# Channel attention with a gelu FFN: v's splits one per step through DRAM, the seven-product scheme in first steps, softmax in finer pieces

## The chip, the cores and the metric

One core of one Trainium2 chip. The metric is the device time of one execution in microseconds; the time of a kernel is the median of several runs. All arithmetic is float32: every product of the main loops is made in three TensorE passes over operands split in a high and a low part (hi x hi, hi x lo, lo x hi), in the type fp32r.

## The reference

```python
B, N, C = 4, 6080, 256; d_ff = 2048
qn = q / (norm(q, axis=1) + 1e-6);  kn = k / (norm(k, axis=1) + 1e-6)   # per channel, over all N
s = kn.transpose(0, 2, 1) @ qn / tau                                    # 256 x 256 per batch
a = softmax(s, axis=-1)
x = (v @ a).reshape(B * N, C)
out = gelu(x @ w_in) @ w_out
```

## The kernel before, in words

**The algebra.** The 256 x 256 matrix a is folded into w_in: per batch, w = a @ w_in (256 x 2048) is made once, and the main loop does gelu(v @ w) @ w_out. v comes transposed (channels on the partitions).

**Groups and steps.** The main loop has 24 groups (b, p): batch b of 4, pair p of 6, each of two blocks of n tokens (n = 512, 480 for p = 5). A group has NU = 8 steps u, each for 256 of the 2048 columns of w. "First step" means u = 0, "second step" u = 1, "border" the change from one group to the next. A step's *first products* are the 2 x 2 block product v @ w in seven products of 128 x 128 with 128 x n (Winograd's form of Strassen's scheme, `first_products`, called do0 to do6 in the order `ORDER`, line 542). They go into two PSUM banks, h0 and h1, in turn; ScalarE copies two partial sums (p1, p5) and u2, VectorE adds them (h<-h,u and h<-h,p), and ScalarE applies gelu: twice per block (gh, rounded, and g, full), VectorE giving gl = g - gh.

**Second products.** gelu's result times w_out is a step late: while step i does its first products, the second products of step i-1 go in between, three matmuls after each do. In a step of the scheme (`strassen`, line 555, which leaves out u = 0) two of gelu's four blocks are kept whole in x, `sums` (line 586) forms the sums of blocks from it on VectorE (x<-x), ScalarE casts them to gh1 (768 columns) and gh0 (1024), VectorE makes gl1 and gl0, and the second products are 12 matmuls of 512 columns and 21 of 256 into the banks c10, c11, c00, p0, p1 and c01. After a plain step (u = 0) they are 24 of 512 columns into c10, c11, c00 and c01. With the 21 first matmuls of 512 that is 33 + 21 small, or 45.

**The end of a group.** Over eight steps the banks add up. c10 and c11 are copied out in the last second products. Then `combine` (line 763) takes p0 and p1 out (a ScalarE copy osb<-p, two VectorE osb<-p,osb, two osb<-osb,p) and `merge` (line 778) adds c00 and c01 to that (osb<-c,osb) and stores. Until merge 0 has read c00, the next group can't write there.

**What sets the order.** From group (0,1) on each of PE, VectorE and ScalarE keeps the program's order (`InOrder`, line 129). A table of jobs, `at(step, slot, job)`, puts side work behind the do of a slot (0 to 5), behind a step's products (6) or behind everything (EDGE = 8). The side work is:
- for the next group's v: `load_v`, four sums of its blocks (`v_sum`, line 516), and seven splits (`v_split`, ScalarE's cast vh, VectorE's vl = v - vh), straight into the operands that the next group's products read. An operand is free when the product of the same number in the last step has read it, so the splits of before stand in the last step and in the next group's first step (line 984);
- for the next batch: loads and splits of q and k (`split_qk`, hl<-raw,hl), their products in bursts of 8 matmuls added to sacc, the norms, and `softmax` (line 341) in the steps 36 to 39 of each batch's 48, followed by `w_part` (a @ w_in, 12 matmuls) and `w_split` (weight sums hl<-hl, wh, wl) in the steps 41 to 50;
- for each step: loads of wo and ws (w_out in two parts, and its sums) two steps and one step ahead (`ahead`, line 899).

All DMAs are issued by SP, in program order.

Of the kernel before, what the change touches and what calls it, by code (L numbers as in the profile page):

```python
# [17 lines left out]
P = 128  # L18
# [47 lines left out]
def channel_attention_gelu_ffn(ctx, tc, qk, kqt, vt, tau, w_in, w_out, out):  # L66
# [274 lines left out]
    def softmax(first):  # L341
# [39 lines left out]
        dve.reciprocal(out=r, in_=z)  # L381

# [121 lines left out]
    def load_v(b, p):  # L504
        t0, n = PAIRS[p]
        raw = pv.tile([P, NCT, 2 * NT], F32, name="v_raw")
        nc.sync.dma_start(out=raw[:, :, :2 * n],
                          in_=vt[:, b * N + t0:b * N + t0 + 2 * n].rearrange("(t p) n -> p t n", p=P))
        vraw[b, p] = raw
# [6 lines left out]
    def v_sum(b, p, i):  # L516
        n = PAIRS[p][1]
        x = v_blocks(b, p)
        if i == 0:
            vts[b, p] = [pv.tile([P, NT], F32, name=f"vs{k}") for k in range(4)]  # L520
        ts = [t[:, :n] for t in vts[b, p]]
        to, x0, x1 = ((0, x[0, 1], x[0, 0]), (2, x[1, 1], x[0, 1]), (1, x[1, 1], ts[0]), (3, x[1, 0], ts[1]))[i]
        dve.tensor_tensor(out=ts[to], in0=x0, in1=x1, op=ALU.subtract)

    def v_split(b, p, i):
# [3 lines left out]
        if (b, p) == (0, 0) and i == B12:  # L529
            src = x[0, 1]  # L530
        if src is None:
            src = vts[b, p][i - T1][:, :n]
# [22 lines left out]
    def strassen(b, p, u):  # L555
        return u > 0 and (b, p) > (0, 1) and (b, p, u) != (B - 1, NP - 1, NU - 1)
# [106 lines left out]
    def plain_products(b, p, u):  # L663
# [9 lines left out]
        for j in (1, 0):  # L673
# [14 lines left out]
    def second_products(b, p, u, blocks):  # L688
# [89 lines left out]
    def merge(b, p, c):  # L778
# [4 lines left out]
        parts = ((0, n // 2), (n // 2, n)) if last and c == NCT - 1 else ((0, n),)  # L783
        for lo, hi in parts:
# [78 lines left out]
    for i in (B11, B21, B12, B22):  # L863
        deque(v_split(0, 0, i), 0)
# [49 lines left out]
    for b in range(1, B):  # L914
        start, num, den = (8, 5, 2) if b == 1 else (4, 14, 5)
# [16 lines left out]
    EDGE = 8  # L932

    for (b, k), s in bursts.items():
# [10 lines left out]
        for m in range(NCT):  # L945
            at(s + m, EDGE, lambda b=b, k=k, m=m: burst(b, k, m))
# [5 lines left out]
    for b in range(1, B):  # L952
        base = (b - 1) * NP * NU
        for i in range(2 * NCT * NSC):

            def norm(b=b, i=i, step=base + 8 + i):
# [3 lines left out]
                at(step + 1, 2, lambda: next(gen, None))  # L960
            at(base + 8 + i, EDGE, norm)

        def soft(step=base + 36):
            gen = softmax(False)
            next(gen)
            spread(gen, step, 12, 10 + EDGE, 22, 26, 20 + EDGE)
        at(base + 36, EDGE, soft)
        for g in range(NWG):
            at(base + 39 + 2 * g, EDGE if g == 0 else EDGE + 1, lambda b=b, g=g: load_win(b, g))
            for m in range(NCT):  # L970
                at(base + 41 + 2 * g + m, EDGE, lambda b=b, g=g, m=m: w_part(b, g, m))
# [4 lines left out]
    for b in range(B):  # L976
        for p in range(NP):
            nxt = (b, p + 1) if p + 1 < NP else (b + 1, 0)
            base = (b * NP + p) * NU
            if nxt[0] < B:  # L980
                at(base + 1, EDGE, lambda nxt=nxt: load_v(*nxt))
                for i in range(4):
                    at(base + 3 + i, 6, lambda nxt=nxt, i=i: v_sum(*nxt, i))
                for i, (hi, lo) in enumerate(((1, 2), (2, 3), (3, 4), (5, 6), (6, 10), (10, 11), (11, 12))):

                    def vs(nxt=nxt, i=i, step=base + NU - 1, lo=lo):
                        gen = v_split(*nxt, ORDER[i][1])
                        next(gen)
                        spread(gen, step, lo)
# [83 lines left out]
```

## Time and profile before

| | |
|---|---|
| median of 3 runs | 2174.5 us (2173.92 to 2175.94) |
| the profiled execution | 2174.69 us |
| its span, first to last instruction | 2172.9 us |
| mean granted TensorE clock | 1.00 |
| PE, PEld, DVE, ACT, POOL busy | 99%, 84%, 80%, 75%, 0% |
| chain that ended last, by engine | PE 87%, DVE 7%, ACT 4%, issue 1% |
| DMA | 352.18 MB, mean 162 GB/s |

PE is TensorE's matmul stream, PEld its weight loads (beside it), DVE VectorE, ACT ScalarE, SP the engine that issues the DMAs. All times are microseconds from the start of the span. A row of the timeline has start, duration, engine, line, operation and the names out<-in; the line is 138 for nearly all, as one helper issues everything, so rows are told apart by their tiles. A row of the windows has a stretch of time, its length, and the busy time and instruction count of PE, PEld, DVE, ACT and POOL in it, then the granted clock, the share of DMA time and GB/s. In a row of groups stand the count, the busy time, and the mean of one in nanoseconds; in a row of DMA issues the count, the size of one and the median time to landing. The durations of neighbouring instructions on one engine overlap a little: what one adds to a queue is the distance of starts, its pitch.

### The profile page before, as it was taken

How to read it: one execution, taken by the hardware profiler on the slowest of the kernel's cores; microseconds unless marked ns; L12 is line 12 of the kernel's file. 1: busy time of each engine (PE TensorE's matmuls, PEld its weight loads, DVE VectorE, ACT ScalarE, POOL GpSimd, SP SyncE). 2: the span in 40 equal slices, each digit the busy share in tenths (PEclk: the TensorE clock that was granted, in tenths of full speed). 3: DMA queues.
4: the chain of work that ended last, by engine and by line, in shares of the span. 5: the costliest groups of instructions: out<-in, count | busy, mean ns of one | idle time of the engine just before them, and what ended most of it. 6: DMA issues, size and time to landing. Idle time of an engine off the chain costs nothing.

```text
span 2172.9 us, 29906 instructions
## 1 busy us (share of the span) xinstructions
PE 2152.8 (99%) x11061; PEld 1822.7 (84%) x11061; DVE 1734.9 (80%) x2732; ACT 1622.5 (75%) x2692; POOL 1.3 (0%) x8
## 2 busy tenths in 40 slices
PE   9999999999999999999999999999999999999999
PEld 8777888887888888888888888888888888888888
DVE  6997788877788788887788878888778777777776
ACT  5767778867777787786777778887677777677675
POOL 0000000000000000000000000000000000000000
PEclk9999999999999999999999999999999999999999
DMA  9545655544344555553434545554344333333332
GB/s 381 180 150 199 213 184 199 183 161 146 136 144 145 176 204 180 199 202 128 140 135 141 173 168 202 184 205 163 106 146 144 118 129 114 127 128 115 125 119 95
DMA packets 100547, 352.18 MB, mean 162 GB/s; under 512 B 10288, under 2 KB 12464, under 8 KB 98352
## 3 DMA queue, kind: packets, MB, share of 16 engines
q1 hardware_dynamic: 100400, 350.27, 46.3%
q8 instruction: 87, 1.43, 0.3%
q14 instruction: 60, 0.49, 0.1%
HBM read 312.74 MB, written 37.49 MB: 161 GB/s over the span
## 4 chain that ended last, share of the span: by engine, by line
PE 87%; DVE 7%; ACT 4%; issue 1%; DMA 0%; DVEq 0%; ACTq 0%; POOL 0%; POOLq 0%
PE h L138 45%; PE c L138 33%; PE p L138 9%; DVE h L138 2%; DVE vl L138 2%; DVE x L138 1%; ACT gh L138 1%; DVE gl L138 1%; ACT x L138 1%; ACT vh L138 1%; ACT g L138 0%; DVE small L138 0%; ACT L138 0%; ACT p L138 0%; DVE osb L138 0%
## 5 line engine op out<-in xcount | busy, mean ns | idle before, releaser
L138 PE MATMUL c<-gh,wo 128*128 128x512 f32 (+3 forms) x2460 | 870.4, 364 | 0.4 <-DVE wo L138 0.4
L138 PE MATMUL h<-vh,wh 128*128 128x512 f32 (+1 forms) x1312 | 520.3, 397 | 12.9 <-DVE h L138 2.8
L138 PEld LDWEIGHTS c<-gh,wo 128*128 128x128 f32 x2460 | 462.2, 188 | 81.9 <-DVE wo L138 1.5
L138 PE MATMUL h<-vh,wl 128*128 128x512 f32 (+1 forms) x1312 | 513.5, 391 | 0.0
L138 PE MATMUL h<-vl,wh 128*128 128x512 f32 (+1 forms) x1312 | 513.5, 391 | 0.0
L138 ACT ACTIVATE gh<-h 128x512 fp32r<-128x512 f32 (+1 forms) x446 | 277.9, 623 | 238.2 <-DVE h L138 219.2
L138 PE MATMUL c<-gl,wo 128*128 128x512 f32 (+3 forms) x1230 | 443.8, 361 | 0.1
L138 DVE TENSOR_TENSOR gl<-x,gh 128x768 fp32r<-128x768 f32 (+3 forms) x306 | 329.8, 1078 | 63.5 <-ACT gh L138 63.3
L138 DVE TENSOR_TENSOR gl<-g,gh 128x512 fp32r<-128x512 f32 (+1 forms) x462 | 314.5, 681 | 49.3 <-ACT g L138 47.1
L138 DVE TENSOR_TENSOR h<-h,p 128x512 f32<-128x512 f32 (+1 forms) x368 | 251.4, 683 | 79.5 <-PE h L138 68.3
L138 ACT COPY p<-h 128x512 f32<-128x512 f32 (+1 forms) x368 | 213.7, 581 | 126.3 <-PE h L138 126.2
L138 PEld LDWEIGHTS h<-vh,wh 128*128 128x128 f32 x1312 | 247.0, 188 | 72.3 <-ACT p L138 9.2
L138 ACT CAST gh<-x 128x768 fp32r<-128x768 f32 (+3 forms) x306 | 286.8, 937 | 16.7 <-DVE x L138 11.7
L138 PEld LDWEIGHTS h<-vh,wl 128*128 128x128 f32 x1312 | 246.4, 188 | 51.9
L138 DVE TENSOR_TENSOR x<-x 128x256 f32<-128x256 f32 (+4 forms) x491 | 241.1, 494 | 52.5 <-ACT x L138 34.8
L138 PEld LDWEIGHTS h<-vl,wh 128*128 128x128 f32 x1312 | 246.7, 188 | 35.4
L138 ACT ACTIVATE g<-h 128x512 f32<-128x512 f32 (+1 forms) x446 | 271.6, 609 | 0.0
L138 PEld LDWEIGHTS c<-gl,wo 128*128 128x128 f32 x1230 | 231.0, 188 | 45.3 <-DVE gl L138 0.5
L138 ACT ACTIVATE x<-h 128x512 f32<-128x512 f32 (+1 forms) x306 | 182.3, 609 | 48.9 <-DVE h L138 47.8
L138 PE MATMUL p<-gh,ws 128*128 128x256 f32 (+1 forms) x918 | 210.2, 280 | 0.0
L138 DVE TENSOR_TENSOR h<-h,u 128x512 f32<-128x512 f32 (+1 forms) x184 | 125.8, 684 | 83.5 <-PE h L138 82.6
L138 PEld LDWEIGHTS p<-gh,ws 128*128 128x128 f32 x918 | 162.6, 189 | 6.8
(153 smaller groups left out, 2229.5 us busy)
## 6 DMA issues: line engine op xcount, KB each, us to landing
wo<-keep_out SPq DMA_DIRECT2D x184, 512.0 KB, 4.5
ws<-keep_sum SPq DMA_DIRECT2D x153, 512.0 KB, 3.7
raw<-qk SPq DMA_DIRECT2D x94, 512.0 KB, 4.5
raw<-kqt SPq DMA_DIRECT2D x72, 512.0 KB, 4.6
v_raw<-vt SPq DMA_DIRECT2D x20, 1024.0 KB, 5.0
out<-osb SPq DMA_DIRECT2D x40, 512.0 KB, 3.9
hl<-keep_in SPq DMA_DIRECT2D x12, 1024.0 KB, 5.4
raw<-w_in SPq DMA_DIRECT2D x8, 512.0 KB, 6.9
```

The lines of the kernel that those rows point to most:

```text
L138: r = op(*args, **kw)
```

## The change

**v through DRAM, one operand per step.** In step i of a group (i = 0 to 6) the operand ORDER[i] of the next group is split: ScalarE's cast into a buffer vp behind do5, VectorE's subtraction (in place, into v_raw or vs) behind do3 of the next step (for i = 0 behind do6), and two DMAs store both parts in DRAM. In the group's last step `v_fetch` loads operand i into vh and vl behind do i. The four sums stand in the steps 0, 2, 3 and 4 and the buffer v_raw is loaded a group earlier; group (0,0) does this for (0,1) too.

**The scheme in first steps.** `strassen` no longer leaves out u = 0, in the groups from (0,2) on, so that all 8 steps of 22 groups use it. Then c01's first products write only half of the bank, and `merge` of c01 adds that half. `combine` and `merge` move: the combine's two halves to slots 1 and 2 of the second step, merge 0 to slot 2, merge 1 to slot 3.

**Softmax in finer pieces, border work ahead of the last groups.** `softmax` yields at two more places, and its pieces stand at the slots 2, 3, 7 (step 37), 2, 5, 6 (step 38) and 7 (step 39). A new slot EARLY = 7 lies after do6 and ahead of the second products that are still left (p1 and c01): bursts, w_part and the softmax's matmuls go there, where they stood behind all of them. The second products of a scheme step are ordered c00, c00, p0, p0, p1, p1, c01 (c00, p0, c00, p1, p1, p0, c01 before). The norms move to steps with few q and k splits, and the first bursts start one step earlier.

```diff
     def strassen(b, p, u):
-        return u > 0 and (b, p) > (0, 1) and (b, p, u) != (B - 1, NP - 1, NU - 1)
+        return (b, p) > (0, 1) and (b, p, u) != (B - 1, NP - 1, NU - 1)
...
         dve.reciprocal(out=r, in_=z)
+        if not first:
+            yield
...
+        if not first:
+            yield
+        for m in range(NCT):
             dve.reduce_max(out=nms[:, m:m + 1], in_=ts[m], axis=AX.X, negate=True)
...
+        hi = pv.tile([P, NT], F32R, name="vp", bufs=2)
+        act.copy(out=hi[:, :n], in_=f32(src))
+        yield
+        dve.tensor_tensor(out=src, in0=f32(src), in1=f32(hi[:, :n]), op=ALU.subtract)
+        to = keep_v[p % 2][i]
+        nc.sync.dma_start(out=to[:, 0, :n], in_=f32(hi[:, :n]))
+        nc.sync.dma_start(out=to[:, 1, :n], in_=f32(src))
+
+    def v_fetch(b, p, i):
...
+        nc.sync.dma_start(out=f32(hi[:, :n]), in_=keep_v[p % 2][i][:, 0, :n])
+        nc.sync.dma_start(out=f32(lo[:, :n]), in_=keep_v[p % 2][i][:, 1, :n])
...
+        if c == NCT - 1 and all(strassen(b, p, u) for u in range(NU)):
+            parts = ((n // 2, n),)
...
-            at(s + m, EDGE, lambda b=b, k=k, m=m: burst(b, k, m))
+            at(s + m, EARLY, lambda b=b, k=k, m=m: burst(b, k, m))
...
-            spread(gen, step, 12, 10 + EDGE, 22, 26, 20 + EDGE)
-        at(base + 36, EDGE, soft)
+            spread(gen, step, 12, 13, 10 + EARLY, 22, 25, 26, 30 + EARLY)
+        at(base + 36, 2, soft)
...
-                for i, (hi, lo) in enumerate(((1, 2), (2, 3), (3, 4), (5, 6), (6, 10), (10, 11), (11, 12))):
+                for i, (step, slot) in enumerate(((0, 6), (2, 0), (3, 0), (4, 0))):
+                    at(base + step, slot, lambda nxt=nxt, i=i: v_sum(*nxt, i))
+                for i, (_, x) in enumerate(ORDER):
...
+                        spread(gen, step, 16 if i == 0 else 13)
+                    at(base + i, 5, vs)
+                fetch = [(i, i) for i in range(7)]
...
-                        spread(gen, step, 1)
+                        spread(gen, step, 2)
                         for c in range(NCT):
-                            at(step, 2, lambda c=c: merge(b, p, c))
-                    at(base + NU + 1, 0, end)
+                            at(step, 2 + c, lambda c=c: merge(b, p, c))
+                    at(base + NU + 1, 1, end)
```

Three places of the engines' orders show what moved. The first is VectorE in the second step of group (1,3): osb<-p and osb<-osb are the combine of the group before, osb<-c00 and osb<-c01 its merges, gl the low parts of gelu, sacc a burst's sum, hl the split of q and k, h<-h0,u2 what do3's gelu needs. Before:

```order
L138 TENSOR_TENSOR gl1_8918<-g_8919,gh1_8917 128x512
L138 TENSOR_TENSOR sacc_6603<-h0_8950,sacc_6603 128x512
L138 TENSOR_TENSOR gl0_8933<-g_8934,gh0_8932 128x512
L138 TENSOR_TENSOR osb_8973<-p0_8187,osb_8973 128x256
L138 TENSOR_TENSOR osb_8973<-p1_8202,osb_8973 128x256
L138 TENSOR_TENSOR osb_8973<-osb_8973,p1_8202 128x256 x2
L138 TENSOR_TENSOR osb_8973<-c00_8086,osb_8973 128x512
L138 TENSOR_TENSOR osb_8973<-c01_8098,osb_8973 128x512
L138 TENSOR_TENSOR hl_8987<-raw_8830,hl_8987 128x1024
L138 TENSOR_TENSOR h_9007<-h0_8977,u2_8994 128x512
```

After, with vs a sum of the next v:

```order
L138 TENSOR_TENSOR vs_9386<-v_raw_9278 128x512
L138 TENSOR_TENSOR x_9353<-x_9353 128x512
L138 TENSOR_TENSOR x_9353<-x_9353 128x256 x2
L138 TENSOR_TENSOR gl1_9389<-x_9353,gh1_9388 128x768
L138 TENSOR_TENSOR gl0_9391<-x_9353,gh0_9390 128x1024
L138 TENSOR_TENSOR osb_9427<-p0_8498,osb_9427 128x256
L138 TENSOR_TENSOR osb_9427<-p1_8511,osb_9427 128x256
L138 TENSOR_TENSOR hl_9425<-raw_9276,hl_9425 128x1024
L138 TENSOR_TENSOR osb_9427<-osb_9427,p1_8511 128x256 x2
L138 TENSOR_TENSOR osb_9427<-c00_8483,osb_9427 128x512
L138 TENSOR_TENSOR h_9447<-h0_9414,u2_9434 128x512
```

The scheme's x sums and its two wide gl now stand ahead of the combine, the hl split has moved from behind the merges to between the combine's halves, and h<-h0,u2 still follows merge 0, with merge 1 behind it.

The second is ScalarE in the same step, from its last gelu on; p1, p5 and u2 are the copies of the first products. Before:

```order
L138 ACTIVATE g_8934<-h1_8835 128x512
L138 COPY p1_8966<-h1_8962 128x512
L138 COPY osb_8973<-p0_8187 128x256
L138 COPY p5_8981<-h0_8977 128x512
L138 CAST hl_8987<-raw_8830 128x1024
L138 COPY u2_8994<-h1_8962 128x512
```

After:

```order
L138 ACTIVATE x_9353<-h1_9281 128x512
L138 CAST gh1_9388<-x_9353 128x768
L138 COPY p1_9406<-h1_9402 128x512
L138 CAST gh0_9390<-x_9353 128x1024
L138 COPY p5_9418<-h0_9414 128x512
L138 CAST hl_9425<-raw_9276 128x1024
L138 COPY osb_9427<-p0_8498 128x256
L138 COPY u2_9434<-h1_9402 128x512
```

The copy osb<-p0 that starts the combine was ahead of p5 and hl, and is behind both and behind the two casts gh1 and gh0.

The third is ScalarE around the exponentials (t0, t1) of batch 2's softmax, with the two table loads that they need. Before:

```order
L138 COPY p5_10470<-h0_10466 128x512
L138 COPY u2_10479<-h1_10455 128x512
L138 ACT_TABLE_LOAD
L138 ACTIVATE t0_10329,small_10328<-t0_10329,small_10328 128x256
L138 ACTIVATE t1_10331,small_10328<-t1_10331,small_10328 128x256
L138 ACT_TABLE_LOAD
L138 ACTIVATE gh_10492<-h_10490 128x512
L138 ACTIVATE g_10494<-h_10490 128x512
```

After:

```order
L138 ACTIVATE gh_11015<-h_11012 128x512
L138 ACTIVATE g_11017<-h_11012 128x512
L138 ACTIVATE x_11032<-h_11029 128x512
L138 CAST vp_11040<-vs_10625 128x480
L138 ACT_TABLE_LOAD
L138 ACTIVATE t0_10761,small_10760<-t0_10761,small_10760 128x256
L138 ACTIVATE t1_10763,small_10760<-t1_10763,small_10760 128x256
L138 ACT_TABLE_LOAD
L138 ACTIVATE x_11032<-h1_10962 128x512
L138 CAST gh1_11062<-x_11032 128x768
```

They were behind the step's copies, ahead of its first gelus; they are now between the last two gelus (x) of a step, behind one v cast.

More of the change, by code (lines that the diff above doesn't have):

```diff
@@ L505, in load_v @@
         t0, n = PAIRS[p]
-        raw = pv.tile([P, NCT, 2 * NT], F32, name="v_raw")
-        nc.sync.dma_start(out=raw[:, :, :2 * n],
+        raw = pv.tile([P, NCT, 2 * NT], F32R, name="v_raw")
+        nc.sync.dma_start(out=f32(raw[:, :, :2 * n]),
                           in_=vt[:, b * N + t0:b * N + t0 + 2 * n].rearrange("(t p) n -> p t n", p=P))
@@ L518, in v_sum, with v_first @@
         x = v_blocks(b, p)
[L519 to L523, printed above, removed]
+        ts = vts.setdefault((b, p), {})
+        to, x0, x1 = ((T1, x[0, 1], x[0, 0]), (T2, x[1, 1], ts.get(T1, x)), (T4, x[1, 0], ts.get(T2, x)),
+                      (T3, x[1, 1], x[0, 1]))[i]
+        x0, x1 = f32(x0), f32(x1 if i in (0, 3) else x1[:, :n])
+        ts[to] = pv.tile([P, NT], F32R, name="vs", bufs=2)
+        dve.tensor_tensor(out=f32(ts[to][:, :n]), in0=x0, in1=x1, op=ALU.subtract)
+    keep_v = [[pdram.tile([P, 2, NT], F32, name=f"keep_v{k}_{i}") for i in range(7)] for k in range(2)]
+    def v_first(i, name):
+        n = PAIRS[0][1]
+        src = v_blocks(0, 0)[{B11: (0, 0), B21: (1, 0), B22: (1, 1), B12: (0, 1)}[i]]
+        hi = pv.tile([P, NT], F32R, name=f"vh{name}")
+        lo = pv.tile([P, NT], F32R, name=f"vl{name}")
+        vops[0, 0, i] = hi, lo
+        act.copy(out=hi[:, :n], in_=f32(src))
+        dve.tensor_tensor(out=lo[:, :n], in0=f32(src), in1=f32(hi[:, :n]), op=ALU.subtract)
     def v_split(b, p, i):
@@ L528, in v_split @@
         src = {B11: x[0, 0], B21: x[1, 0], B22: x[1, 1]}.get(i)
-        if (b, p) == (0, 0) and i == B12:
-            src = x[0, 1]
         if src is None:
-            src = vts[b, p][i - T1][:, :n]
+            src = vts[b, p][i][:, :n]
+        hi = pv.tile([P, NT], F32R, name="vp", bufs=2)
+        act.copy(out=hi[:, :n], in_=f32(src))
+        yield
[4 more added lines that the diff above has]
+    def v_fetch(b, p, i):
+        n = PAIRS[p][1]
         hi = pv.tile([P, NT], F32R, name=f"vh{i}")
@@ L953, in channel_attention_gelu_ffn, with norm @@
         base = (b - 1) * NP * NU
-        for i in range(2 * NCT * NSC):
-            def norm(b=b, i=i, step=base + 8 + i):
+        split_at = {}
+        for k in range(FIRSTB if b == 1 else 0, NQS // NB):
+            for t in range(NB):
+                x = bursts.get((b, k - 1), bursts[b, k] - 3) + 1 + t
+                split_at[x] = split_at.get(x, 0) + 1
+        free = sorted(range(base + (9 if b == 1 else 2), base + 35), key=lambda x: (x % NU == 0, split_at.get(x, 0), x))
+        for i, x in enumerate(sorted(free[:2 * NCT * NSC])):
+            def norm(b=b, i=i, step=x):
                 gen = norm_part(b, *divmod(i, NSC))
@@ L959, in norm @@
                     next(gen)
-                at(step + 1, 2, lambda: next(gen, None))
-            at(base + 8 + i, EDGE, norm)
+                at(step, 2, lambda: next(gen, None))
+            at(x - 1, EDGE, norm)
         def soft(step=base + 36):
```

39 lines of the change are left out of this document (20 added, 19 removed).

## The prediction

> **What bounds the kernel now.** I read the page's busy shares first, then the windows cut at the starts of the 192 steps, then the timelines of the steps that are longer than their matmuls.
>
> ```profile
> span 2172.9 us, 29906 instructions
> PE 2152.8 (99%) x11061; PEld 1822.7 (84%) x11061; DVE 1734.9 (80%) x2732; ACT 1622.5 (75%) x2692; POOL 1.3 (0%) x8
> ```
>
> TensorE is busy 99% of the span, so time is gained only by fewer matmuls or by closing PE's few gaps, and lost wherever a new wait of PE appears. The next rows are step windows: a step in the scheme, a second step of a group (its second products are those of the plain first step), and the sums over all 22 first steps and all 22 second steps of the groups from (0,2) on.
>
> ```profile
> core 0: us, PE busy (x) PEld busy (x) DVE busy (x) ACT busy (x) POOL busy (x), PEclk, DMA share, GB/s
> 1954.23:1964.32 10.09, 10.09 (x57) 8.66 (x55) 7.51 (x12) 7.00 (x12) 0.00 (x0) 1.00 0.30 104
> 1933.71:1944.14 10.43, 10.43 (x47) 8.38 (x46) 8.11 (x14) 7.11 (x13) 0.00 (x0) 1.00 0.51 174
> sum 248.98, PE 244.90 PEld 200.87 DVE 226.87 ACT 222.23 POOL 0.00; mean PE 11.13 PEld 9.13 DVE 10.31 ACT 10.10 POOL 0.00
> sum 240.31, PE 240.30 PEld 196.80 DVE 186.52 ACT 162.10 POOL 0.00; mean PE 10.92 PEld 8.95 DVE 8.48 ACT 7.37 POOL 0.00
> ```
>
> The granted clock is 1.00 in every row. First steps take 248.98/22 = 11.32 us with VectorE busy 10.31 of it; second steps 10.92 with VectorE at 8.48. Where the matmuls of a step start tells the rest:
>
> ```profile
> 1954.23 0.40 PE L138 MATMUL h<-vh,wh 128*128 128x512 f32 x1
> 1954.46 0.40 PE L138 MATMUL h<-vl,wh 128*128 128x512 f32 x1
> 1960.45 0.28 PE L138 MATMUL c<-gh,wo 128*128 128x256 f32 x1
> 1960.56 0.28 PE L138 MATMUL c<-gl,wo 128*128 128x256 f32 x1
> ```
>
> Starts are 0.232 us apart for 512 columns and 0.116 for 256. So 33 x 0.232 + 21 x 0.116 = 10.09 for a scheme step and 45 x 0.232 = 10.44 for a plain one, as the windows have it. The first matmul into c00 comes 1960.45 - 1954.23 = 6.22 us into a step.
>
> **The change part by part.** The sum stands against the profiled execution's own 2174.69 us, 1.8 us more than its span and 0.2 above the median of 2174.5. A measurement of this kernel can tell about 0.2% (4.3 us) from no change.
>
> *1. Scheme in 22 first steps.* Each saves 10.43 - 10.09 = 0.34 us of matmul in the step after it: **-7.6**.
>
> *2. Waits in the first steps.* Their matmuls, counted at 0.232 and 0.116 (0.219 and 0.110 in the 480-column groups, with the bursts), come to 235.65 us; the windows' sum is 248.98. The 13.3 us between are waits behind the v splits that crowd VectorE and ScalarE there. With one split per step they go: **-13.3**. What is late next is the second step.
>
> *3. Waits in the second steps.* This decides. Before, the old group's combine and merge have a plain step's short VectorE queue ahead of them. Now the scheme's sums of the first step stand there. Of a group border of before and of a steady step:
>
> ```profile
> 1954.00 1.61 DVE L138 TENSOR_TENSOR x<-x 128x512 f32<-128x512 f32 x3 [0.75 <-ACT x L138]
> 1955.53 0.95 DVE L138 TENSOR_TENSOR gl<-x,gh 128x768 fp32r<-128x768 f32 x1
> 1956.73 1.23 DVE L138 TENSOR_TENSOR gl<-x,gh 128x1024 fp32r<-128x1024 f32 x1 [0.25 <-ACT gh L138]
> ...
> 886.21 0.88 DVE L138 TENSOR_TENSOR osb<-p,osb 128x256 f32<-128x256 f32 x2 [0.48 <-ACT osb L138]
> 887.13 0.75 DVE L138 TENSOR_TENSOR osb<-osb,p 128x256 f32<-128x256 f32 x2
> 887.92 1.29 DVE L138 TENSOR_TENSOR osb<-c,osb 128x512 f32<-128x512 f32 x2
> 889.12 1.22 DVE L138 TENSOR_TENSOR hl<-raw,hl 128x1024 fp32r<-128x1024 f32 x1
> 890.25 0.69 DVE L138 TENSOR_TENSOR h<-h,u 128x512 f32<-128x512 f32 x1
> ```
>
> In the border of before (its step begins at 884.32) merge 0 ends at 887.92 + 0.69 = 888.61, 4.3 us in, 1.9 ahead of c00's 6.22. In the steady step the last sum, gl of 1024, ends at 1957.96, 3.73 in. In the new order a v sum (0.69) stands ahead of the x sums and fills most of the idle 0.75, so I put gl's end at 3.8 to 4.2. Then the combine (0.88 + 0.75, with pitch 0.92 + 0.79) and merge 0 (0.69) give 4.2 + 0.92 + 0.79 + 0.69 = 6.6: c00 waits 0.4. That is so at 10 of the 21 borders, **+4**.
>
> At 8 borders, (0,3), (0,4), (1,2) to (1,4) and (2,2) to (2,4), a q/k split falls into the second step. VectorE's part (889.12 to 890.25, 1.13) now lies between the halves of the combine, and ScalarE's lies ahead of the copy that the combine needs:
>
> ```profile
> 1955.65 1.05 ACT L138 CAST gh<-x 128x1024 fp32r<-128x1024 f32 x1
> 1956.60 0.58 ACT L138 COPY p<-h 128x512 f32<-128x512 f32 x1
> ...
> 885.80 0.38 ACT L138 COPY osb<-p 128x256 f32<-128x256 f32 x1
> 887.18 1.05 ACT L138 CAST hl<-raw 128x1024 fp32r<-128x1024 f32 x1
> 888.13 0.59 ACT L138 COPY u<-h 128x512 f32<-128x512 f32 x1
> ```
>
> ScalarE: gh cast, p copy, hl cast from 1957.1 (the p copy's start and half a us), 2.9 into the step (3.5 where a burst's sum delays the x sums by 0.6), ending at 3.9 to 4.5, then osb<-p to 4.3 to 4.9. VectorE from there: 0.92, hl 1.13, 0.79, merge 0.69: 7.8 to 8.4. c00 waits 1.6 to 2.2; I take 1.9: **+15**. Below, if the ScalarE copy is no hindrance, 4.2 + 0.92 + 1.13 + 0.79 + 0.69 - 6.22 = 1.5 (12); if VectorE's queue runs 0.5 earlier than I think, 1.0 (8). Above 2.5 (20), since h<-h,u now stands behind merge 0. The second steps' sums say the same: VectorE's 8.48 loses two gl (1.4) and gains x (1.5), both gl (2.1) and v work (0.7), 11.4 in 10.6 us.
>
> At the 3 borders (b,0) four weight sums stand there too:
>
> ```profile
> L138 DVE TENSOR_TENSOR hl<-hl 128x256 f32<-128x256 f32 x64 | 25.1, 421 | 0.4
> L138 DVE TENSOR_TENSOR vl<-vs,vh 128x512 fp32r<-128x512 f32 x76 | 51.9, 685 | 0.0
> 1140.45:1153.17 12.72, 12.12 (x61) 9.46 (x61) 11.70 (x19) 10.93 (x20) 0.00 (x0) 1.00 0.60 210
> 1097.77:1107.63 9.86, 9.86 (x57) 8.76 (x56) 7.89 (x12) 7.32 (x12) 0.00 (x0) 1.00 0.46 170
> ```
>
> Some three of the 0.42 us fall ahead of the combine: 0.4 + 1.2 = 1.6 each, **+5** (0 to 9).
>
> *4. Weight splits (four steps in each of three blocks).* The window of 1140.45 has such a split with the v splits beside it and waited 1.5 us; a step of 480 columns without one has none (9.86). Now one v part (0.69) stands beside each, and w_part, moved ahead of the last groups, needs its bank earlier. From 0 to 1.5 each; I take 0.55, nearer to the quiet row since one split is there, not three: 12 x 0.55 = **+6.6** (0 to 18).
>
> *5. Softmax, three blocks.* Windows and ScalarE around the exponentials before:
>
> ```profile
> 1554.19:1565.82 11.63, 10.80 (x58) 8.92 (x56) 10.23 (x29) 6.56 (x12) 0.00 (x0) 1.00 0.26 92
> 1565.82:1578.68 12.86, 11.27 (x59) 9.07 (x58) 9.06 (x16) 10.52 (x18) 0.00 (x0) 1.00 0.27 93
> 1578.68:1589.63 10.95, 10.48 (x55) 8.70 (x55) 9.31 (x17) 8.70 (x16) 0.00 (x0) 1.00 0.21 84
> 1035.23 1.28 ACT L138 ACT_TABLE_LOAD   x1
> 1036.52 0.51 ACT L138 ACTIVATE t<-t,small 128x256 f32<-128x256 f32 x1
> ...
> 1037.64 1.28 ACT L138 ACT_TABLE_LOAD   x1
> 1038.93 0.63 ACT L138 ACTIVATE gh<-h 128x512 fp32r<-128x512 f32 x1
> ```
>
> Against 10.09 (and 0.25 and 0.4 of softmax matmuls) these steps wait 1.3, 2.4 and 0.9: 4.5 a block. Afterwards the chain of small VectorE operations stays (1.3), the middle step is nearly free (0.2), and the exponentials stand between two gelus at a step's end. From the first load to the next gelu is 1038.93 - 1035.23 = 3.70 us, in which the last gelu's bank is held; the next step's second product needs that bank 1.39 us in (six matmuls), and the gelu would end about 4 in: 2.6, with 0.4 behind it, 3.0. With 0.2 at the transposes 4.7 a block: 3 x 0.2 = **+0.6** (-8 to +6).
>
> The exponential begins 0.01 us after its load. The Trainium skill, ScalarE: Activation LUTs, "What ACT_TABLE_LOAD costs", gives about 1283 ns for the load, as this trace has it, and 1380 ns more of drain for every switch, which these rows do not show; with it the six switches in the exposed place would cost 8.3 us more and the sum would be about 2198.
>
> *6. v through DRAM.* 14 fetches of 256 KB in a group's last step, seven stores of two parts, all in SP's queue, where a fetch waits for the product that frees its buffer and wo and ws stand behind it. The nearest rows, and a first step's DMA:
>
> ```profile
> wo<-keep_out SPq DMA_DIRECT2D x184, 512.0 KB, 4.5
> ws<-keep_sum SPq DMA_DIRECT2D x153, 512.0 KB, 3.7
> out<-osb SPq DMA_DIRECT2D x3, 240.0 KB, 2.0
> 872.58:884.32 11.74, 11.74 (x65) 9.77 (x63) 10.69 (x16) 10.90 (x19) 0.00 (x0) 1.00 0.72 248
> ```
>
> Store and fetch take some 2 + 2 us, and each operand is needed a step (10 us) after its buffer is free, which hides them. All of it is 3.7 MB and wo and ws 1.0: at 248/0.72 = 344 GB/s 13.7 us, while the last operand is needed 18 us after the first fetch. I take 0.7 us at four late borders where a fetch stands behind wo: **+3** (0 to 10). Without cover each border would pay 1 to 2.
>
> *7. Group (0,0).* Its 75.5 us are filled by VectorE:
>
> ```profile
> 67.91:143.40 75.49, 74.88 (x319) 59.19 (x319) 74.86 (x146) 48.59 (x92) 0.00 (x0) 1.00 0.43 151
> ```
>
> The first v sums move into it, up to four of 0.69, less what the step after it loses of its wait: **+1.5** (-0.5 to +3).
>
> Sum: -7.6 - 13.3 + 4 + 15 + 5 + 6.6 + 0.6 + 3 + 1.5 = +14.8; 2174.7 + 14.8 = 2189.5, on the median **2189**.
>
> **The rivals.** *A, the gaps stay closed (faster).* If the combine gets through before c00 (its queue is 2 us shorter than I count, or PE's own earlier pieces give it time), parts 3 and 4 shrink to about 2 us and part 6 to nothing: -20.9 + 0.6 + 1.5 + 2 = -16.8, 2158. For it: VectorE is busy only 80% overall, and the steps of before are gapless at 8.5 of 10.5. Against: VectorE works in order and the order puts the hl split inside the combine. It decides at a merge 0 that ends before 6.2 us. Chance 0.27.
>
> *B, half of it (no change).* Second steps wait only at the split borders, 1.5 each (12), weight splits 0.25 (3), the rest as above without part 6: -20.9 + 12 + 3 + 0.6 + 1.5 + 1.5 = -2, 2172. Chance 0.13.
>
> *C, the fetches bind (slower still).* Every border's first products wait for v because SP stands at a fetch while wo waits: 1 us at 22 borders on top of the forecast, about 2211. It decides when an operand lands later than 10 us after its buffer is free. Against: 344 GB/s does it in 13.7 us. Chance 0.08.
>
> *D, a switch of tables costs more in the new place:* 2198, chance 0.02; the rows speak against it.
>
> **How the numbers follow.** The forecast's own mechanism, slower by waits in the second steps, has 0.50; with the low ends of its terms (part 3 at 12, weight splits 2, no DMA) it is 2179, with the high ends of two terms 2206. Slower: 0.50 + 0.08 + 0.02 = 0.60; same 0.13; faster 0.27. The range 2155 to 2206 takes in most of A; below it and above it lie about 0.1 each.
>
> **What would show it.** Right: second steps of 10.09 us in matmuls that last 10.5 (quiet) and 12 (with a q/k split, bursts apart), PE idle before the first c00 of a group and released by VectorE's osb<-c; first steps at 10.1. A loss of about 3 us in the step after the exponentials. Wrong: second steps at 10.1 throughout (then A), PE released by a DMA of vh or vl at the borders (then C), first steps still over 10.5, or waits in the weight-split steps above 1 us.

## The result and the profile after

The changed kernel takes 2260.0 us (median; 2255.2 to 2263.6) where the kernel before takes 2175.1 beside it: 1.039 times as long, 95% interval 1.037 to 1.041. The prediction said slower, 2189, with 2206 as the upper end of its range: the sign was right, the size was not, by 71 us. The profiled execution has a span of 2256.5 us, 83.6 more than before.

The page after, first its span and busy times, then all its DMA:

```profile
span 2256.5 us, 31701 instructions
PE 2173.1 (96%) x11259; PEld 1831.4 (81%) x11259; DVE 1779.3 (79%) x2798; ACT 1636.2 (73%) x2692; POOL 1.3 (0%) x8
DMA packets 196463, 530.86 MB, mean 235 GB/s; under 512 B 20944, under 2 KB 37456, under 8 KB 194256
```

PE's share fell from 99% to 96%: the time went into waits of PE, no engine became the bound. There are 51% more bytes (352.18 to 530.86 MB). The windows of the 22 first steps, then of the 22 second steps, each as the sum:

```profile
sum 277.82, PE 251.28 PEld 204.39 DVE 188.53 ACT 183.58 POOL 0.00; mean PE 11.42 PEld 9.29 DVE 8.57 ACT 8.34 POOL 0.00
sum 269.14, PE 244.98 PEld 203.40 DVE 229.11 ACT 177.20 POOL 0.00; mean PE 11.14 PEld 9.25 DVE 10.41 ACT 8.05 POOL 0.00
```

First steps were to lose their 13.3 us of waits. VectorE's load there did fall as the change meant (10.31 to 8.57 a step), and yet they got longer, from 248.98 to 277.82. Second steps went from 240.31 to 269.14, with VectorE at 10.41 where it was at 8.48.

I take a step's wait as its length less its matmuls at the spacings of the prediction (0.232, 0.116, 0.219 and 0.110 us); time lost by a lower clock counts as a wait in it. The difference of the two spans then adds up:

| where | waits before | after | forecast change | measured |
|---|---|---|---|---|
| first steps of groups (0,2) on | 13.3 | 42.1 | -13.3 + 3 | +28.8 |
| second steps | 0.5 | 35.5 | +24 | +35.0 |
| weight splits, in (b,5) and steps 2 and 3 of (b,0) | 0.4 | 9.2 | +6.6 | +8.8 |
| softmax, steps 36 to 39 | 13.6 | 13.2 | +0.6 | -0.3 |
| group (0,1) | 1.7 | 13.4 | | +11.7 |
| group (0,0), whole length | 93.6 | 98.5 | +1.5 with (0,1) | +4.9 |
| all else | 0.5 | 2.3 | 0 | +1.8 |
| matmuls saved | | | -7.6 | -7.6 |
| sum | | | +14.8 | +83.1 |

Three places hold 65 of the 68 us that the forecast lacks: the first steps (39), the two first groups (15) and the second steps (11).

**First steps.** PE at do3 and at the start of do4 in the first step of (3,1), which begins at 1831.26; in brackets what it waited for:

```profile
1835.42 0.39 PE L138 MATMUL h<-vh,wh 128*128 128x512 f32 x1
1837.06 0.50 PE L138 MATMUL h<-vl,wh 128*128 128x512 f32 x1 [1.25 <-DMA vl<-keep_v]
...
1839.10 0.47 PE L138 MATMUL h<-vh,wh 128*128 128x512 f32 x1 [0.63 <-DMA vh<-keep_v]
```

It waits for fetches. SP's queue shows when these were issued; the last step before it runs from 1821.17 to 1831.26:

```profile
1825.19 0.43 SPq L562 DMA_DIRECT2D vl<-keep_v  x1
1826.92 0.32 SPq L561 DMA_DIRECT2D vh<-keep_v  x1
1831.46 0.32 SPq L300 DMA_DIRECT2D wo<-keep_out  x1
1831.83 0.42 SPq L562 DMA_DIRECT2D vl<-keep_v  x1
```

From 1826.92 to 1831.46 SP issues nothing. It stands at wo, the weights of the next group's first step, whose buffer is read until the step's last products. For the first 1.2 of these 4.5 us it could not have gone on anyway, as the end of this part shows. The fetch of do3's second part and all behind it go out late, by 3.8 us as the run that moves this wo will show, and the one issued at 1831.83 lands when do3 has stood for 1.4 us, 5.2 us after its issue. The page's rows of issues have the store and the two fetches (KB each, median us to landing):

```profile
keep_v<-vp SPq DMA_DIRECT2D x133, 256.0 KB, 2.9
vh<-keep_v SPq DMA_DIRECT2D x133, 256.0 KB, 5.9
vl<-keep_v SPq DMA_DIRECT2D x133, 256.0 KB, 5.8
```

The windows of this last step and of the first step behind it say why that takes so long (the last two columns are DMA's share and GB/s):

```profile
1821.17:1831.26 10.09, 10.09 (x56) 8.66 (x55) 7.73 (x12) 7.36 (x13) 0.00 (x0) 1.00 0.99 377
1831.26:1844.79 13.53, 11.10 (x57) 8.52 (x55) 8.10 (x13) 8.08 (x14) 0.00 (x0) 1.00 0.84 281
```

The 16 DMA engines are busy 99% of the last step, at 377 GB/s. And SP never has more than eight transfers on the way: none of its 1293 issues from the ninth on starts before the transfer eight places ahead of it has landed, and 100 of them (30 of 627 in the kernel before) go out within 0.12 us of that landing, SP having stood until then. SP's waits show it where a fetch (lines 561 and 562) waits for the landing of a load that it has no use for (us in total, times, longest):

```profile
SPq L561 <- DMA wo<-keep_out: 14.0, 14, 1.5
SPq L562 <- DMA ws<-keep_sum: 8.2, 9, 1.0
```

So a slow landing also delays what is issued next. In the example the ws eight places ahead landed at 1828.16, and only from there on was it wo's buffer alone that held SP. Eight transfers of 256 KB at 377 GB/s take 5.6 us (an estimate), about the landing time of a fetch.

**Second steps.** VectorE in the second step of (1,2), from 827.57, a border with a q/k split:

```profile
830.64 1.23 DVE L138 TENSOR_TENSOR gl<-x,gh 128x1024 fp32r<-128x1024 f32 x1 [0.25 <-ACT gh L138]
832.34 0.89 DVE L138 TENSOR_TENSOR osb<-p,osb 128x256 f32<-128x256 f32 x2 [0.47 <-ACT osb L138]
833.15 1.21 DVE L138 TENSOR_TENSOR hl<-raw,hl 128x1024 fp32r<-128x1024 f32 x1
834.28 0.74 DVE L138 TENSOR_TENSOR osb<-osb,p 128x256 f32<-128x256 f32 x2
835.06 0.69 DVE L138 TENSOR_TENSOR osb<-c,osb 128x512 f32<-128x512 f32 x1
```

and PE's first product into c00 there:

```profile
835.80 0.38 PE L138 MATMUL c<-gh,wo 128*128 128x256 f32 x1 [1.85 <-DVE osb L138]
```

This is the forecast chain: gl ends 4.3 us into the step, the combine waits for ScalarE's copy, the split stands in its middle, merge 0 ends 8.2 in, and c00 starts 2.0 late.

**The exponentials** stand where the prediction had them, at the step's end. ScalarE's second table load, and the gelu behind it:

```profile
1086.50 1.28 ACT L138 ACT_TABLE_LOAD   x1
1087.80 0.60 ACT L138 ACTIVATE x<-h 128x512 f32<-128x512 f32 x1
```

PE's next product into the bank that this gelu reads:

```profile
1088.45 0.50 PE L138 MATMUL h<-vh,wh 128*128 128x512 f32 x1 [2.46 <-ACT x L138]
```

PE loses 2.6 us there. The gelu follows its table load by 0.02 us, so no further drain shows behind the load here either, and rival D is out.

### The profile page after: what moved, and what is told of

It is laid out like the page before. It is cut to its first block, busy times and chain, and to the rows that moved or that the text cites. A ratio compares the mean times of both kernels' runs of the same rounds, so it can differ in the third digit from the quotient of the medians.

```text
span 2256.5 us, 31701 instructions
## 1 busy us (share of the span) xinstructions
PE 2173.1 (96%) x11259; PEld 1831.4 (81%) x11259; DVE 1779.3 (79%) x2798; ACT 1636.2 (73%) x2692; POOL 1.3 (0%) x8
## 2 busy tenths in 40 slices
DMA packets 196463, 530.86 MB, mean 235 GB/s; under 512 B 20944, under 2 KB 37456, under 8 KB 194256
## 4 chain that ended last, share of the span: by engine, by line
PE 75%; DMA 9%; DVE 8%; ACT 5%; issue 2%; SPq 1%; DVEq 0%; ACTq 0%; POOL 0%; POOLq 0%
PE h L138 39%; PE c L138 26%; PE p L138 9%; DMA vl<-keep_v 4%; DVE x L138 2%; DVE h L138 2%; DVE osb L138 2%; ACT gh L138 1%; DMA keep_v<-vs 1%; DMA wo<-keep_out 1%; DMA vh<-keep_v 1%; DMA raw<-kqt 1%; DVE gl L138 1%; DVE hl L138 1%; ACT x L138 1%
## 5 line engine op out<-in xcount | busy, mean ns | idle before, releaser
L138 PE MATMUL c<-gh,wo 128*128 128x512 f32 (+3 forms) x2372 | 828.9, 360 | 21.9 <-DVE osb L138 20.0
L138 PE MATMUL h<-vh,wh 128*128 128x512 f32 (+1 forms) x1312 | 520.3, 397 | 33.7 <-DMA vh<-keep_v 14.5
L138 PE MATMUL h<-vl,wh 128*128 128x512 f32 (+1 forms) x1312 | 519.2, 396 | 11.9 <-DMA vl<-keep_v 10.2
L138 ACT ACTIVATE gh<-h 128x512 fp32r<-128x512 f32 (+1 forms) x402 | 251.4, 625 | 296.4 <-DVE h L138 279.5
L138 DVE TENSOR_TENSOR gl<-x,gh 128x768 fp32r<-128x768 f32 (+1 forms) x350 | 377.0, 1077 | 43.5 <-ACT gh L138 43.2
L138 DVE TENSOR_TENSOR x<-x 128x256 f32<-128x256 f32 (+2 forms) x557 | 275.1, 496 | 113.1 <-ACT x L138 100.3
L138 ACT CAST gh<-x 128x768 fp32r<-128x768 f32 (+1 forms) x350 | 327.8, 937 | 34.7 <-DVE x L138 29.9
L138 DVE TENSOR_TENSOR gl<-g,gh 128x512 fp32r<-128x512 f32 (+1 forms) x418 | 283.7, 680 | 31.2 <-ACT g L138 29.2
L138 ACT ACTIVATE x<-h 128x512 f32<-128x512 f32 (+1 forms) x350 | 212.0, 607 | 60.2 <-DVE h L138 54.1
L138 ACT ACTIVATE g<-h 128x512 f32<-128x512 f32 (+1 forms) x402 | 245.1, 610 | 0.0
L138 PE MATMUL p<-gh,ws 128*128 128x256 f32 (+1 forms) x1050 | 242.8, 281 | 0.0
L138 PEld LDWEIGHTS p<-gh,ws 128*128 128x128 f32 x1050 | 187.5, 191 | 7.9
```

What stands on the lines that cost most here:

```text
L138: r = op(*args, **kw)
```

## The experiments

**The scheme alone.** The kernel before with first steps in the scheme, and nothing else:

```diff
-        return u > 0 and (b, p) > (0, 1) and (b, p, u) != (B - 1, NP - 1, NU - 1)
+        return (b, p) > (0, 1) and (b, p, u) != (B - 1, NP - 1, NU - 1)
```

> The kernel before with one part of the change alone: the scheme in first steps (and merge 1 on half of c01). v stays in SBUF, combine and merges at their old slots, the q/k split behind the merges. Theory (the loss comes from where combine, fetches and bursts were put, not from the scheme): 7.6 us of matmuls go, the first steps keep their 13 us of waits, and merge 0, with only the x sums ahead of it, ends about 5.5 us into the second step, before c00 at 6.2, so that second steps wait under 10 us in all: 2168 to 2178 us. Rival (the scheme in a first step is itself too much for VectorE at a border): second steps wait 1 to 2 us at each of 22 borders, 2185 to 2200.

2189.8 us, ratio 1.0065 (1.005 to 1.008), as the rival had it. The sums of its windows, first and second steps:

```profile
sum 247.45, PE 243.69 PEld 201.98 DVE 229.04 ACT 220.22 POOL 0.00; mean PE 11.08 PEld 9.18 DVE 10.41 ACT 10.01 POOL 0.00
sum 254.68, PE 240.52 PEld 200.64 DVE 213.91 ACT 167.53 POOL 0.00; mean PE 10.93 PEld 9.12 DVE 9.72 ACT 7.62 POOL 0.00
```

The second steps are 14.4 us longer although 7.6 us of matmuls left them: 22 us of waits. Here c00 waits 0.3 to 1.2 us at 14 borders, and at seven of the eight with a split, where it stands behind the merges, c00 does not wait and PE stands 1.26 us at do5, for h<-h,u behind the split.

**The order on VectorE, twice.** First the combine and merge 0 one slot earlier, ahead of the split; then the split two slots later, out of the combine:

```diff
-                        spread(gen, step, 2)
+                        spread(gen, step, 1)
                         for c in range(NCT):
-                            at(step, 2 + c, lambda c=c: merge(b, p, c))
-                    at(base + NU + 1, 1, end)
+                            at(step, 1 + 2 * c, lambda c=c: merge(b, p, c))
+                    at(base + NU + 1, 0, end)
...
-                at(step, 2, lambda: next(gen, None))
-            at(prev + 1 + t, 1, split)
+                at(step, 4 if step % NU == 1 else 2, lambda: next(gen, None))
+            at(prev + 1 + t, 3 if (prev + 1 + t) % NU == 1 else 1, split)
```

> The changed kernel with combine and merge 0 one slot earlier (0, 1 and 1 instead of 1, 2 and 2), which puts them ahead of the q/k split and the combine's first half ahead of the widest gl. Theory (the 35.5 us that second steps wait are the order on VectorE): they fall below 12, about 2235 us. Rival (VectorE is full there whatever the order, and the wait goes to p0 or to the next step): under 8 us gained, over 2250.

> The changed kernel with the q/k splits that fall into second steps two slots later (ScalarE behind do3, VectorE behind do4), out of the combine. Theory (half of the wait before c00 is that split, half the sums ahead of it): at the 8 borders with such a split c00 waits 0.4 us as at the quiet ones, not 2.0; the other parts of the second step keep their waits, so that all second steps fall from 35.5 to 20 to 25: 2245 to 2250 us. Rival (VectorE is full, as the earlier combine showed): the 1.6 us come back at do5 or in the next step, over 2255.

2255.3 (2251.9 and 2258.7) and 2257.7 (2255.3 and 2260.1), against 2255 to 2264 for the changed kernel: the rival in both. Second steps still wait 32.6 and 31.4 us. PE at the border of (1,2) with the earlier combine:

```profile
835.14 0.38 PE L138 MATMUL c<-gh,wo 128*128 128x256 f32 x1 [0.48 <-DVE osb L138]
836.87 0.50 PE L138 MATMUL h<-vh,wh 128*128 128x512 f32 x1 [0.78 <-DVE h L138]
```

c00's wait shrinks from 2.0 to 0.65, and 0.9 comes up at do5, where h<-h,u is now late. With the late split c00 waits only 0.4, as expected, and the bursts that need the split wait instead, up to 3.4 us. VectorE has 10.4 us of work in these steps and several readers with a date; each of the two orders tried made another of them late.

**Plain first steps** in the changed kernel (the first diff turned round):

> The changed kernel with plain first steps as before; v through DRAM, softmax, bursts, combine slots stay. Theory (the second steps wait for merge 0 because the x sums and the wide gl of a scheme step fill VectorE ahead of it): second steps fall from 35.5 us of waits to under 8, 7.6 us of matmuls come back, the first steps keep about 40: 2235 to 2240 us. Rival (it is the later slots of combine alone): over 20 us of waits stay in the second steps, 2250 or more.

Second steps fall from 35.5 to 16.2 us of waits, more than half, but not to under 8 as expected: 1.4 stay at the borders where the split sits inside the combine. First steps rise to 46 us: at the end of 11 of them PE waits 1.34 us for a gelu behind a burst or a w_part (see the two first groups). And the matmuls come back: 2253.3 (2248.7 and 2257.9). The theory was right on the second steps in the main and missed the time, which is the rival's.

**Fewer bytes.** A quarter, then a half of the columns of each fetch, from group (0,3) on; the rest of each operand is set to zero, so most of these products are left out in value:

```diff
+        m = n if (b, p) < (0, 3) else n // 4
+        if m < n:
+            nc.gpsimd.memset(f32(hi[:, m:n]), 0.0)
+            nc.gpsimd.memset(f32(lo[:, m:n]), 0.0)
+        nc.sync.dma_start(out=f32(hi[:, :m]), in_=keep_v[p % 2][i][:, 0, :m])
+        nc.sync.dma_start(out=f32(lo[:, :m]), in_=keep_v[p % 2][i][:, 1, :m])
```

> The changed kernel with v's fetches of a quarter of the columns from group (0,3) on (the rest of each operand is set to zero by GpSimd, so three quarters of the products of these groups are left out in value; the number and order of all DMAs stay). Theory (bytes: 3.7 MB of fetches beside wo, ws and v_raw fill the DMA engines at a border): the waits of first steps, 42 us now, fall below 12, about 2228 us. Rival (order: a fetch stands in SP's queue behind a wait for something else): the waits stay over 30 us, 2248 or more.

> As the kernel with v's fetches of a quarter, with half of the columns fetched and the other half of each operand set to zero by GpSimd from group (0,3) on. Theory (bytes, with a limit): 1.8 MB of fetches and 1.0 of wo and ws fit into a step's 10 us at 350 to 400 GB/s, so first steps wait little more than with a quarter (1.9 us), under 10: 2215 to 2225 us. Rival (a wait proportional to bytes): half of the way, about 20 us of waits, 2235.

2214.1 (ratio 1.018, 1.016 to 1.020) and 2221.6 (one run). With a quarter, the sum of the first steps:

```profile
sum 237.54, PE 236.89 PEld 203.29 DVE 187.58 ACT 181.63 POOL 0.00; mean PE 10.77 PEld 9.24 DVE 8.53 ACT 8.26 POOL 0.00
```

and its row of issues:

```profile
vl<-keep_v SPq DMA_DIRECT2D x119, 64.0 KB, 3.8
```

With a half, the same two:

```profile
sum 241.70, PE 238.20 PEld 202.97 DVE 187.47 ACT 181.53 POOL 0.00; mean PE 10.83 PEld 9.23 DVE 8.52 ACT 8.25 POOL 0.00
```

```profile
vl<-keep_v SPq DMA_DIRECT2D x119, 128.0 KB, 4.7
```

Waits of 1.9 and 6.0 us, from 42.1. But both runs changed more than the bytes. The number of DMAs is the same, their order in SP's queue is not: the wo that SP stands at comes later in both. At the borders into (3,1) to (3,4) it stood ahead of do3's second part, and now it stands behind that and two stores; at 14 others it has one to four fetches more ahead of it; only into (0,2) and the (b,0) is its place the same. So these two runs do not tell bytes from place. What remains in them shows the rest of the change by itself: with a quarter, c00 waits 0.36 to 0.40 us at the borders into (3,1) to (3,4), 2.0 at those with a split, 1.4 at (b,0).

**Another queue** for the fetches, with GpSimd issuing them:

> The changed kernel with v's fetches issued by GpSimd, which is idle, instead of SP; bytes, order among themselves and all else stay. Theory (bytes): the same 3.7 MB leave for the same 16 DMA engines, the first steps keep 30 us or more of waits, and the time stays within 15 us of 2260. Rival (order in SP's queue, a fetch in front of wo and ws or behind a store's wait): first steps fall under 15 us of waits, 2230 or less.

2295.3 (one run), 35 us slower still; first steps wait 73.6 us, and a fetch lands in 8.1:

```profile
vh<-keep_v POOLq DMA_DIRECT2D x133, 256.0 KB, 8.1
```

So it did not tell place from bytes: the other issuer brought a slower path with it. The Trainium skill, DMA: Bandwidth & Descriptors, "Issuing engines are not separate DMA queues", says that DMAs of all issuers run on the same 16 engines and interleave; the landing, longer and not shorter, agrees.

**The place in SP's queue, at the same bytes.** The description of the kernel before says that SP issues in program order; the traces show otherwise. The program asks for the wo of a first step at the end of the step u = 6, ahead of all fetches of the last step; in the trace it stands behind 7 to 10 of the 14 at 19 of the 22 borders. Here it is asked for a step later, and the trace has it behind all 14 at these 19:

```diff
+        if u == NU - 1 and (b, p) != (0, 0) and after(1)[0] < B:
+            load_wo(after(1))
-        if nxt[0] < B and nxt[:2] != (0, 0):
+        if nxt[0] < B and nxt[:2] != (0, 0) and (u != NU - 2 or (b, p) == (0, 0)):
             load_wo(nxt)
```

> The changed kernel with the load of wo for a group's first step issued a step later, behind v's fetches in SP's queue instead of between them; bytes and all else stay. In the changed kernel SP stands at that wo until the products of the last step are done (in group (3,0)'s last step from 1827.2 to 1831.5), and the fetches behind it go out 4.6 us late. Theory 1 (bytes alone): first steps keep over 30 of their 42 us. Theory 2 (the place in SP's queue and the bytes together: late by 4.6 us, and then 5 to 6 us to landing instead of 2 to 3): the fetches go out 4 us earlier, the first steps fall under 15 us of waits, 2225 to 2235 us.

2230.2 (ratio 1.0255, 1.0236 to 1.0274): 30 us gained by one load. The sum of its first steps:

```profile
sum 244.94, PE 241.13 PEld 202.75 DVE 187.56 ACT 182.15 POOL 0.00; mean PE 10.96 PEld 9.22 DVE 8.53 ACT 8.28 POOL 0.00
```

its fetches in the rows of issues:

```profile
vl<-keep_v SPq DMA_DIRECT2D x133, 256.0 KB, 5.5
```

and SP from the last step of (3,0) on, which runs from 1805.67 to 1815.77:

```profile
1811.35 0.32 SPq L561 DMA_DIRECT2D vh<-keep_v  x1
1812.56 0.32 SPq L562 DMA_DIRECT2D vl<-keep_v  x1
...
1819.94 0.42 SPq L300 DMA_DIRECT2D wo<-keep_out  x1
```

do3's second part is issued 6.9 us into the last step, not 10.7, and first steps wait 9.3 us, not 42.1, with all the bytes and landings of 5.5 us. So the place of one load accounts for 33 of the 42 us. The eight issues from 1811.35 to 1816.90 each start 0.01 to 0.07 us after the landing of the transfer eight places ahead: with wo out of the way, the landings pace the queue. Of the 9.3 us that stay with all the bytes, 7.4 are not there with a quarter of them, though wo stands no further back in that run. What fewer bytes alone do, with wo in its old place, was not tried. Second steps wait 40 us here, 5 more.

**v in SBUF as before**, the rest of the change kept:

> The changed kernel with v's sums and splits as before, straight into the operands in SBUF, in the last and the first steps; all else stays. Theory (separate places): first steps go back to about 13 us of waits (from 42) and the groups (0,0) and (0,1) give back some 8 of their 17 us, while the second steps keep their 35: 2220 to 2230 us. Rival (the traffic through DRAM delays everything, wo, ws and the q/k loads included): second steps and weight splits recover too, 2185 us or less.

2213.8 (ratio 1.017, 1.016 to 1.019), lower than the theory's 2220 to 2230, higher than the rival's 2185. First steps wait 21.6 us, not 13; (0,1) gives back 4.5 us and (0,0) 3.1, together the 8 expected; second steps fall to 22.8, which I had not expected. VectorE has 9.88 us of work in them, not 10.41, and c00 waits 1.4 us at the borders with a split, not 2.0; that the difference is the sum of v ahead of the combine (0.69 us) was not tried by itself.

**The two first groups.** Bursts behind all second products and begun where they were; then only those of (0,1), with the plain products of (0,0) in the old order, a line of the change that I had not weighed:

```diff
-            at(s + m, EARLY, lambda b=b, k=k, m=m: burst(b, k, m))
+            at(s + m, EDGE, lambda b=b, k=k, m=m: burst(b, k, m))
...
-        for j in (0, 1):
+        for j in (1, 0):
```

> The changed kernel with the bursts behind all second products again, and started where the kernel before starts them; w_part and softmax stay in the new slot. Theory (in the plain group (0,1) a burst ahead of the last second product keeps gh0, a single buffer, in use 1.5 us longer; the last gelu, its bank and the next do0 wait for it, 1.33 us in each of four steps): the waits of (0,1) fall from 13.4 to about 8, and bursts in second steps that waited 1 to 2.8 us for a bank lose most of that: 2245 to 2253 us. Rival (the seven v splits with their stores fill the engines in (0,1)): 13 us stay there, 2256 or more.

> The changed kernel with two things as before in the groups (0,0) and (0,1) alone: the order of the plain products of (0,0) (column blocks 1, 0), which the change had turned round, and the bursts of (0,1) behind all second products. Theory (three causes for the 17 us there: the turned order, 1.7 us at the start of (0,1) and about 2 in (0,0); bursts ahead of the last second product, 1.33 us in four steps; and v's splits and stores, the rest): the waits of (0,1) fall from 13.4 to 6 to 7, (0,0) gets 1 to 2 us shorter, about 2252 us. Rival (splits and stores alone): no change.

What a burst ahead of the last second product does in a plain step, in the changed kernel's (0,1), on ScalarE:

```profile
216.65 0.60 ACT L138 ACTIVATE gh<-h 128x512 fp32r<-128x512 f32 x1 [1.41 <-PE c L138]
217.15 0.59 ACT L138 ACTIVATE g<-h 128x512 f32<-128x512 f32 x1
```

and on PE:

```profile
213.54 1.69 PE L138 MATMUL h<-hl 128*128 128x512 f32 x8
...
216.23 0.39 PE L138 MATMUL c<-gh,wo 128*128 128x512 f32 x1
217.79 0.50 PE L138 MATMUL h<-vh,wh 128*128 128x512 f32 x1 [1.18 <-ACT g L138]
```

The burst (213.54) pushes the last product that reads gh0 back, the gelu that needs gh0's only buffer waits for that, and do0 for the gelu: 1.33 us in each of four steps. Both runs take these away and gain little by it, against the 2255 to 2264 of the changed kernel: 2252.6 (2250.7 and 2254.5) and 2257.1 (2254.2 and 2260.0). With all bursts moved, (0,1) keeps 13.7 us, not 8 as expected: the waits for the gelu go, and others for VectorE's h come, up to 4.6 us. Second steps fall by 11 us and first steps rise by 7, of which 5.7 in (0,2). With those of (0,1) moved, that group waits 5.6 us, about as expected, but (0,0) gets 1.6 longer, not shorter, and a step of (0,2) stands still, because ScalarE waits for a load:

```profile
277.05 1.06 ACT L138 ACTIVATE raw<-raw 128x1024 f32<-128x1024 f32 x1 [5.79 <-DMA raw<-kqt]
```

The wait moved to the next late load. What the turned order costs or gains was not told apart.

**A version that beats both.** The kernel before, with only the operands of v through DRAM that were split in first steps, first three, then four of them and not in the groups with a softmax or in (0,1), then with wo behind the fetches. The core of it:

```diff
+                    times = ((1, 2), (2, 3), (3, 4))
+                    for k, x in enumerate((B22, T3, B21, T4)):
...
+                        at(base + 3 + k, 5, vst)
+                    for i in range(3, 7):
+                        at(base + NU - 1, i, lambda nxt=nxt, i=i: v_fetch(*nxt, ORDER[i][1]))
```

> The kernel before (plain first steps, old softmax, old bursts) with only those three operands of v stored in DRAM and fetched that were split in first steps, T3, B21 and T4, from group (0,2) on; the other four are split in the last step as before. Theory (bytes): six fetches are 1.6 MB, with wo and ws 2.6 MB in a step, under what the queue moved (400 GB/s), so they land in time, first steps lose 10 of their 13 us of waits and no other step gains any: 2163 to 2168 us. Rival (any fetch at a border comes late, or the extra stores hold up wo and ws): 2174 us or more.

> As the kernel with three operands through DRAM, with B22 as a fourth, one split per step in steps 3 to 6, and with the way of the kernel before in the groups where the three cost something: (0,1) and the groups that hold a softmax, (b,4) of the first three batches. Theory: first steps where it applies wait under 0.2 us, together 13.3 falls to about 5, softmax and (0,1) are as before: 2166 to 2170 us. Rival (what first steps of before wait for is not those splits but something else on ScalarE and VectorE, since three operands gained only 3 us there): 2174 or more.

> The kernel with four operands through DRAM and the same move of wo. Theory 1: no change against 2169. Theory 2: the few waits for vl that it had in first steps (1.3 us in (3,2), 0.2 to 0.4 elsewhere) go, 2165 to 2168 us.

Three: 2179.7, ratio 1.0020 (1.0011 to 1.0029), the rival's side. First steps gained only 3 us, and the splits cost 3.6 in the softmax steps and 2.7 in (0,1). Four, with these groups spared: 2169.3, 0.9971 (0.9959 to 0.9982). With wo behind the fetches 2165.9, 0.9960 (0.9947 to 0.9974). These two intervals overlap; in the profiled executions the first steps are 3.3 us shorter with wo behind, which agrees with the place. First and second steps of this last one:

```profile
sum 239.23, PE 238.39 PEld 201.64 DVE 196.09 ACT 198.00 POOL 0.00; mean PE 10.84 PEld 9.17 DVE 8.91 ACT 9.00 POOL 0.00
sum 239.50, PE 239.50 PEld 196.50 DVE 195.00 ACT 161.10 POOL 0.00; mean PE 10.89 PEld 8.93 DVE 8.86 ACT 7.32 POOL 0.00
```

First steps wait 3.6 us instead of 13.3, second steps none.

## Why the prediction was right in its sign and wrong in its size

- *Part 1, the scheme (-7.6):* right; and the scheme alone loses (+14.5 us with the old v path), since its second steps wait 22 us.
- *Part 2, waits of first steps (-13.3):* the waits on VectorE and ScalarE did go (1.9 us left with a quarter of the bytes). The step said what is late next, "the second step". That was incomplete: the fetches were late too.
- *Part 3, second steps (+24):* the mechanism and its sizes were right. c00 was forecast to wait 1.9 us at eight borders and waits 2.0; 1.6 at (b,0), and waits 1.4; 0.4 at the ten quiet ones, and waits 0.4 to 0.5 at five of them and 0.1 or nothing at the five of batch 3, whose first steps are late themselves. Of the 11 us above, 8.5 are bursts that wait for their bank (1.1 and 2.8 us at two borders) and a lower clock behind the waits (4.6 us).
- *Part 4, weight splits (+6.6, measured +8.8):* the forecast had 0.55 in each of twelve steps. It is 0.57 in two of the steps of 480 columns in each block and nothing in most others, and waits of 0.9 and 0.8 that were not forecast stand in the third step of (1,0) and (2,0), one of 0.9 in that of (3,0).
- *Part 5, softmax (+0.6, measured -0.3):* 4.4 us a block, forecast 4.7.
- *Part 6, v through DRAM (+3, measured 42 us of waits):* this step failed. It named the mechanism, a fetch behind wo, and then priced it at 0.7 us in four borders, and it excluded the bytes with a sum: 4.7 MB at 344 GB/s take 13.7 us "while the last operand is needed 18 us after the first fetch". The sum counted from the first fetch as if SP never stood still and as if each operand had the last one's date. Its rate was not the fault: 377 GB/s were moved. Ahead of (3,1) SP issues nothing for 4.5 us, the last 3.3 of them for wo alone; 33 of the 42 us go when that one load is moved; and SP never has more than eight transfers on the way. In (3,1), do3's second part has 3.8 us from its issue to its product and takes 5.2; over all a fetch takes 5.8 at up to 99% DMA, not the "2 + 2" of the quiet rows. Its upper end of 10 us rested on the same sum.
- *Part 7, groups (0,0) and (0,1) (+1.5, measured +16.6):* only v sums were counted. The bursts ahead of the last product (5.3 us) were counted as free, though moving them was part of the change, and the splits and stores in (0,1) cost 4.5 us there and 3.1 in (0,0), by the kernel with v in SBUF. The rest was not told apart.
- *Rival C* was the case that came: fetches that bind, though it had wo wait behind a fetch, and here the fetches wait behind wo. It had 0.08 and 1 us a border; measured are 1.9. Its argument against was the sum of part 6.

## What to carry to other kernels

Where a queue of DMAs is issued in order, follow it entry by entry, in the order of the trace, for what each waits for before it may go out: its buffer, and here also the landing of the transfer eight places ahead. Count a transfer's time from there. One load whose buffer is free late cost 30 us here, and moving that load brought them back at the same bytes. Take a landing time from rows with the traffic that the change makes: under that traffic 256 KB took 5.8 us, where the quiet row of 240 KB had 2.0. See in the trace that an experiment changed only what it was meant to change: fewer bytes also moved a load in the queue here. When an engine's work in a step nears the step's length, another order may only change who waits, as both orders tried here did; work taken out of the step shortened the wait in both runs that did so.

## What the hardware showed that was not expected

The granted clock is 1.00 in all 192 steps before. After, seven steps are lower; the first and the last of them:

```profile
244.23:261.57 17.34, 13.88 (x53) 10.70 (x53) 9.18 (x17) 8.81 (x15) 0.00 (x0) 0.90 0.79 278
1467.59:1483.01 15.42, 13.69 (x65) 11.14 (x63) 9.32 (x14) 8.91 (x14) 0.00 (x0) 0.89 0.91 305
```

Length times what the clock lacks, 17.34 x 0.10 and so on, gives 10.2 us over the seven: an eighth of the loss. In the trace's record of the clock these are six drops to 0.50, for 3.4 us each, and each starts 0.2 to 1.9 us behind an idle gap of PE of 1.6 to 2.6 us. The drops start at 254.96, 452.94, 930.80, 1302.86, 1395.02 and 1476.93, which is 58, 140, 109, 27 and 24 times 3.413 us apart, as if the clock were decided once in such a stretch. In the stretch ahead of a drop PE is idle for 1.86 to 2.26 us in five cases and 1.64 in one; the three gaps of 2.46 us at the exponentials each fall into two stretches, at most 1.82 us into one, and leave the clock at 1.00. The two ranges overlap, so the exact limit stays open, and that the waits bring the drops on is argued from this and not shown by a run. The Trainium skill, TensorE: Matmul & The Clock Gate, "HAM oscillation — how this bites in real kernels", has the clock fall after idle gaps of more than about 3.4 us; the longest gap of PE in this trace is 2.63 us, so here shorter gaps were enough.
